# An mLSTM cell followed by a two-layer quick-GELU block: a copy placed ahead of a gelu on ScalarE, and two of GpSimd's adds given to VectorE

## The chip, the cores and the metric

The kernel runs on one core of a Trainium2 chip. The metric is the device time of one execution in microseconds; the time given for a kernel is the median of its runs.

## What is computed

An mLSTM cell runs over 768 steps for 4 batches of 8 heads of size 40. Its output becomes a matrix x of 3072 tokens by 320, which goes through two matrix products with a gelu between them:

```
h_tilde = einsum(C, q);  y = sigmoid(o_gate) * h_tilde / max(|n.q|, 1)      # C, n: the states with decay
x = y as (B*S, H*D)                                                        # 3072 x 320
h = x @ w_in                                                               # 320 x 2048
g = h * sigmoid(1.702 * h)
out = g @ w_out                                                            # 2048 x 320
```

All data are float32.

## The kernel before

**Stages.** The 768 steps are cut into six chunks of 128 steps, w = 0 to 5; a chunk has 4 x 128 = 512 tokens. For each chunk the loop at L929 runs a first product with its gelu (hidden features, up), and then a second product (down), into which the attention work of the next chunk is placed by a hand-written table (`attention`, L918). The order of the instructions on each engine is the order in which the program issues them: the schedule is manual, no planner moves anything. Each engine works through its own list in that order, and waits where an operand or a buffer isn't free.

**The first product.** Chunk 0 uses plain products (`up`, L614). Chunks 1 to 5 use `up_fast` (L707), which does a two-by-two block product with seven products in place of eight (a Strassen-Winograd form). The 2048 hidden features are eight pairs j = 0 to 7 of two rows of 128. For a pair, PE makes seven products of 256 columns (L722), each recorded as two matmuls: 14 for a pair. Their results lie in four PSUM banks: `p1`, `p56` (parts that are shared by the rows) and `row0`, `row1`. The rest of the inner dimension (the last 64 of 320) comes by `row_product` (L701); pairs 0 and 4 issue these matmuls for four pairs at once: their own, j + 2, j + 3 and then j + 1. A row is finished with its last matmul: for pairs 0 and 4 that is the first row product behind the pair, for odd pairs the pair's last L722, and for pairs 2 and 6 the rows are made ahead of `p1` and `p56`.

What happens to a pair's results:

- ScalarE copies the left half of `p1` into a buffer `parts` (L761), called the pair's part here. `parts` has two buffers, used in turn.
- VectorE makes the shared sums: `u2` (L762), a sum into `parts` (L763), a second sum into `parts` (L774).
- VectorE adds `row1` and `parts` into the second row of the pair's `g` (L775).
- The first row of `g`: in pairs 0 to 5 (`apart`) ScalarE copies `row0` into it (L739), and GpSimd adds the parts to it in place (L781), both inputs in SBUF. In pairs 6 and 7 VectorE adds from PSUM (L783).
- ScalarE applies the gelu in place, second row first and then the first row (`gelu_fast`, L688 to L690). This is issued one pair later: `up_fast(w, j)` issues the gelu of pair j - 1.

ScalarE's list in a pair is thus: the part (L761), the gelu of the pair in front (two L690), and the row copy (L739). In pair 2 alone the copy stands ahead of the part.

**Banks.** PSUM's eight banks are a pool of four single banks (`ps_m`) and a pool of two double ones (`ps_a`). The single ones go round: pair 4's `row0` and `row1` use the banks that pair 5 takes for `p1` and `p56`, and pair 5's rows use those that pair 6 takes for `p1` and `p56`. So a pair's `p1` waits for the row copy L739 of the pair in front, and its `p56` for that pair's L775. Rows of pairs 2, 3, 6 and 7 lie in the double banks.

**Other work in the same stage.** VectorE transposes blocks of k and q for the next chunk (L394: two behind pair 1, one behind pair 3, three behind pair 4, two behind pair 5). GpSimd makes differences of `g` for the fast second product (`hidden_difference`, L812, from pair 2 on; `hidden_sums`, L820 and L823, from pair 6 on). In chunk 1 alone GpSimd also makes four sums of the second product's weights (`weight_sums`, L803), one behind each of pairs 0 to 3. SyncE's queue loads the next chunk's v and k (L120).

**The second product.** `down_fast` (L831) makes seven products for half a chunk with PE (L844), sums up on VectorE (L847, L849), and makes late sums (L829). Its second product needs the gelus of pairs 4 to 7. Behind its fourth product, the next chunk's state product (L602) runs; it needs GpSimd's scaled values (L588), which need a column that ScalarE makes behind the last gelu. Later come the scores (L459, weighted on VectorE in L462) and the values (L503).

Of the kernel before, what the change touches and what calls it, by code (L numbers as in the profile page):

```python
# [12 lines left out]
OP = mybir.AluOpType  # L13
# [13 lines left out]
def kernel(  # L27
# [36 lines left out]
    op = ctx.enter_context(tc.tile_pool(name="op", bufs=2))  # L64
# [5 lines left out]
    V, A, G, T = nc.vector, nc.scalar, nc.gpsimd, nc.tensor  # L70
# [266 lines left out]
    def banks(name):  # L337
        return ps_a.tile([128, 2, 512], FP, tag="a", name=name)
# [349 lines left out]
    def gelu_fast(w, j):  # L688
        for i in (1, 0):
            A.activation(out=gs[w, j][:, i, :], in_=gs[w, j][:, i, :], func=AF.Gelu_apprx_sigmoid)  # L690
# [3 lines left out]
    def row_product(w, j, start):  # L694

        n = 2 if w == NW - 2 or (w == NW - 3 and j < 2) else 1
        for h in range(n):
            t = slice(h * W // n, (h + 1) * W // n)
            for i, row in enumerate(row_banks[w, j]):
                r = slice(i * 64, i * 64 + 64)  # L700
                T.matmul(row[:, t], w_in_x[r, j, :], xT[w][r, 2].rearrange("p b t -> p (b t)")[:, t],  # L701
                         start=(start and h == 0), stop=(not start and h == n - 1))

    def bank(name="p_h"):
        return ps_m.tile([128, W], FP, tag="m", name=name)

    def up_fast(w, j):  # L707

        x = temps[w]
        k = j % 4
        left, right = slice(0, half_w), slice(half_w, W)
        f = lambda c, i: w_in_sb[:, c, (2 * j + i) * 128:(2 * j + i + 1) * 128]

        def product(n, out, start, stop):
            a = {1: lambda: f(0, 0), 2: lambda: f(1, 0), 3: lambda: s_in[:, 2, j], 4: lambda: f(1, 1),  # L720
                 5: lambda: s_in[:, 0, j], 6: lambda: s_in[:, 1, j], 7: lambda: f(0, 1)}[n]()
            T.matmul(out, a, x[n], start=start, stop=stop)  # L722

        def row_0():
            product(2, row0[:, left], k == 0, False)
            product(3, row0[:, right], False, k > 0)

        def row_1():
            product(4, row1[:, left], k == 0, False)
            product(7, row1[:, right], False, k > 0)  # L730

        y = work.tile([L, 2, DM + 64], FP, tag="y", name="parts").rearrange("p a b -> p (a b)")
        u2 = second[w]
        g = gs[w, j] = gp.tile([128, 2, W], FP, tag="g", name="g")
        apart = j < NF // 2 - 2

        def copy_row():
            if apart:
                A.copy(out=g[:, 0, :], in_=row0)  # L739

        if k == 2:
            row0, row1 = row_banks[w, j]
            row_1()
            row_0()
        p1, p56 = bank(), bank()
        if k == 0:
            row0, row1 = row_banks[w, j] = bank(), bank()
        elif k != 2:
            row0, row1 = row_banks[w, j]
        product(1, p1[:, left], True, True)  # L750
        if k == 0:
            row_0()
        product(5, p56[:, left], True, True)
        product(6, p56[:, right], True, True)
        if k != 2:
            row_1()
        if k % 2:
            row_0()
        if k == 2:
            copy_row()  # L760
        A.copy(out=y[:, left], in_=p1[:, left])  # L761
        V.tensor_tensor(out=u2, in0=p56[:, right], in1=y[:, left], op=OP.add)  # L762
        V.tensor_tensor(out=y[:, 2 * half_w:3 * half_w], in0=p56[:, left], in1=u2, op=OP.add)  # L763
        if k == 0:
            row_product(w, j, False)
            for n in (2, 3):
                both = banks("p_h")
                row_banks[w, j + n] = both[:, 0, :], both[:, 1, :]
                row_product(w, j + n, True)
            row_banks[w, j + 1] = bank(), bank()  # L770
            row_product(w, j + 1, True)
        if j:
            gelu_fast(w, j - 1)
        V.tensor_tensor(out=y[:, half_w:2 * half_w], in0=row1[:, right], in1=u2, op=OP.add)  # L774
        V.tensor_tensor(out=g[:, 1, :], in0=row1, in1=y[:, half_w:3 * half_w], op=OP.add)  # L775
        u = y.rearrange("p (a t) -> p a t", t=half_w)[:, 0:3:2]
        g0 = g[:, 0, :].rearrange("p (a t) -> p a t", a=2)
        if apart:
            if k != 2:
                copy_row()  # L780
            G.tensor_tensor(out=g0, in0=g0, in1=u, op=OP.add)  # L781
        else:
            V.tensor_tensor(out=g0, in0=row0.rearrange("p (a t) -> p a t", a=2), in1=u, op=OP.add)  # L783

# [144 lines left out]
    for w in range(NW):  # L929
# [24 lines left out]
        else:  # L954
            token_sums(w)
            for j in range(NF // 2):
                up_fast(w, j)
                if more and j == 0:
                    gates(w + 1)
                    load(w + 1, "o")  # L960
                    if w == 1:
                        wait_for(ends[w + 1])
                if w == 1 and j < 4:
                    weight_sums(j)
                if more and j == 2:
                    columns_in(w + 1)
                    spread(w + 1)
                    load(w + 1, "vk")
                if more and j:
                    for n in ((0, 2), (), (4,), (6, 1, 3), (5, 7), (), ())[j - 1]:  # L970
                        block_transposes(w + 1, n)
                if more and j == 7:
                    columns_turn(w + 1)
                if 2 <= j < 6:
                    hidden_difference(w, j - 2)
                if j >= 6:
                    hidden_sums(w, (j - 6,), G)
# [54 lines left out]
```

## Time and profile before

| what | us |
|---|---|
| median of 3 runs (465.45 to 466.07) | 465.86 |
| the profiled execution | 465.77 |
| its span | 464.1 |
| PE busy | 456.6 (98%) |
| VectorE busy (DVE in the profile) | 349.2 (75%) |
| ScalarE busy (ACT) | 185.8 (40%) |
| GpSimd busy (POOL) | 162.8 (35%) |
| L781, GpSimd's add of the first row, 30 times | 38.2 |
| L739, ScalarE's copy of the first row, 30 times | 17.5 |
| L690, the gelus, 80 times | 47.8 |

All times in a profile are microseconds from the start of the span. A line of a timeline or of the chain gives the start, the length and then the instruction, "xN" when N of a kind are merged. An answer by stages gives for each stretch its length, the busy time of PE, PEld (weight loads), DVE, ACT and POOL with the number of instructions, then the granted TensorE clock (1.00 is full speed), the DMA engines' share, and GB/s. A line of waits gives who waited for whom, the sum, the number of times and the longest.

### The profile page before, as it was taken

The page shows a single profiled execution, that of the slowest core. Times are in us where ns is not written, and L with a number is a line of the kernel's source. Part 1 is how long each engine was busy: PE and PEld are TensorE (multiplying, and loading weights), DVE is VectorE, ACT ScalarE, POOL GpSimd, SP SyncE. Part 2 cuts the span into 40 slices and gives each one's busy share as a digit, 9 for nine tenths or more (in the row PEclk, how much of TensorE's full clock was granted, in tenths as well). Part 3 has the DMA queues.
Part 4 walks back from the last instruction along what each step waited for, and adds up shares of the span by engine and source line. Part 5 has one row for each costly group of instructions (what it writes and reads, how often), then busy time and mean ns, then how long its engine had stood idle before and what let it go on. Part 6 is the DMA issues. An engine that isn't in the chain of part 4 may idle for free.

```text
span 464.1 us, 12384 instructions
## 1 busy us (share of the span) xinstructions
PE 456.6 (98%) x5071; PEld 391.2 (84%) x5071; DVE 349.2 (75%) x738; ACT 185.8 (40%) x433; POOL 162.8 (35%) x154
## 2 busy tenths in 40 slices
PE   8999999999989999999999999999999999999996
PEld 6867877776859999779999779999888999787996
DVE  6788998799958785888786888787788766553722
ACT  5686779000536700455800354900264910164200
POOL 5101508000797700266800167610157710146200
PEclk9999999999989999999999999999999999999999
DMA  8998999049976025969024978315999305000000
GB/s 169 187 295 187 253 239 204 4 106 198 149 157 78 3 59 123 200 113 189 9 58 107 194 119 162 53 33 125 175 140 156 63 18 140 29 1 1 1 28 30
DMA packets 135561, 52.87 MB, mean 114 GB/s; under 512 B 101984, under 2 KB 131632, under 8 KB 135504
## 3 DMA queue, kind: packets, MB, share of 16 engines
q1 hardware_dynamic: 127136, 50.27, 55.4%
q10 hardware_dynamic: 8048, 1.66, 1.8%
q8 instruction: 40, 0.66, 0.6%
q0 software_dynamic: 320, 0.15, 0.2%
q14 instruction: 17, 0.14, 0.1%
HBM read 44.52 MB, written 7.54 MB: 112 GB/s over the span
## 4 chain that ended last, share of the span: by engine, by line
PE 88%; SPq 4%; DMA 2%; issue 2%; DVE 2%; POOL 1%; ACT 1%; DVEq 0%; POOLq 0%; ACTq 0%
PE p_out L844 33%; PE p_h L722 24%; PE p_out L790 8%; PE p_h L701 7%; PE p_h L626 5%; SPq L122 3%; PE p_c L602 3%; PE p_o L503 2%; PE p_s L459 2%; PE p_i L511 2%; DMA s_in<-in_moe_w_in_dram 2%; PE p_h L635 2%; POOL g L781 1%; SPq L167 0%; PE p_t L386 0%
## 5 line engine op out<-in xcount | busy, mean ns | idle before, releaser
L781 POOL TENSOR_TENSOR g<-g,parts 128x512 f32<-128x512 f32 x30 | 38.2, 1272 | 196.5 <-ACT g L739 187.7
L761 ACT COPY parts<-p_h 128x256 f32<-128x256 f32 x40 | 14.9, 372 | 164.5 <-PE p_h L722 134.1
L844 PE MATMUL p_out<-w_out_sb,g 128*128 128x160 f32 x480 | 68.9, 300 | 0.0
L722 PE MATMUL p_h<-xT,w_in_sb 128*128 128x256 f32 x240 | 66.4, 385 | 2.0 <-ACT g L739 2.0
L844 PEld LDWEIGHTS p_out<-w_out_sb,g 128*128 128x128 f32 x480 | 66.4, 190 | 0.5
L690 ACT ACTIVATE g<-g 128x512 f32<-128x512 f32 x80 | 47.8, 629 | 30.1 <-DVE g L775 19.1
L722 PEld LDWEIGHTS p_h<-xT,w_in_sb 128*128 128x128 f32 x240 | 44.9, 191 | 14.2 <-issue 5.5
L849 DVE TENSOR_TENSOR o_sb<-o_sb,p_out 128x160 f32<-128x160 f32 x70 | 21.4, 317 | 44.2 <-PE p_out L844 43.6
L844 PE MATMUL p_out<-t_sb,s 128*128 128x160 f32 x320 | 47.1, 300 | 0.0
L844 PEld LDWEIGHTS p_out<-t_sb,s 128*128 128x128 f32 x320 | 44.4, 190 | 0.2
L722 PE MATMUL p_h<-t_x,s_in 128*128 128x256 f32 x160 | 42.0, 385 | 0.0
L435 ACT ACTIVATE wt<-wt,cols 128x64 f32<-128x64 f32 x160 | 38.8, 334 | 0.1
L701 PE MATMUL p_h<-xT,w_in_x 64*128 64x512 f32 (+1 forms) x200 | 37.1, 514 | 0.0
L790 PE MATMUL p_out<-w_out_sb,g 128*128 128x320 f32 x128 | 35.7, 436 | 0.0
L722 PEld LDWEIGHTS p_h<-t_x,s_in 128*128 128x128 f32 x160 | 31.0, 194 | 4.4
L762 DVE TENSOR_TENSOR t_x<-p_h,parts 128x256 f32<-128x256 f32 x40 | 16.9, 424 | 20.3 <-PE p_h L722 12.9
L790 PEld LDWEIGHTS p_out<-w_out_sb,g 128*128 128x128 f32 x128 | 23.9, 190 | 9.6
L701 PEld LDWEIGHTS p_h<-xT,w_in_x 64*128 64x128 f32 x200 | 18.5, 186 | 14.9 <-issue 13.9
L739 ACT COPY g<-p_h 128x512 f32<-128x512 f32 x30 | 17.5, 582 | 31.1 <-PE p_h L701 17.5
L626 PE MATMUL p_h<-xT,w_in_sb 128*128 128x256 f32 x128 | 29.6, 384 | 0.0
L775 DVE TENSOR_TENSOR g<-p_h,parts 128x512 f32<-128x512 f32 x40 | 27.6, 691 | 1.4
L626 PEld LDWEIGHTS p_h<-xT,w_in_sb 128*128 128x128 f32 x128 | 23.6, 190 | 5.3 <-issue 2.4
(205 smaller groups left out, 853.6 us busy)
## 6 DMA issues: line engine op xcount, KB each, us to landing
q_sq<-in_q_dram SPq DMA_DIRECT2D x20, 320.0 KB, 10.6
wt<-m_row SPq DMA_DIRECT2D x20, 256.0 KB, 5.4
k_sq<-in_k_dram SPq DMA_DIRECT2D x16, 320.0 KB, 6.0
out_dram<-o_sb SPq DMA_DIRECT2D x24, 160.0 KB, 1.9
eo<-in_o_gate_dram SPq DMA_DIRECT2D x5, 640.0 KB, 7.9
bits<-in_moe_w_in_dram SPq DMA_DIRECT2D x6, 512.0 KB, 11.3
q_sq<-x_row SPq DMA_DIRECT2D x10, 256.0 KB, 3.0
v_st<-in_v_dram SPq DMA_DIRECT2D x14, 160.0 KB, 5.7
```

What stands on the lines that cost most here:

```text
L435: A.activation(out=x[:, h, :], in_=x[:, h, :], func=AF.Exp, scale=-1.0, bias=cols[w][:, c * PH + h:c * PH + h + 1])
L626: T.matmul(ph[j][i][:, t], w_in_sb[:, c, f * 128:(f + 1) * 128], x[:, c, t], start=(first and c == 0 and n == 0), stop=(not first and c == ...
L690: A.activation(out=gs[w, j][:, i, :], in_=gs[w, j][:, i, :], func=AF.Gelu_apprx_sigmoid)
L701: T.matmul(row[:, t], w_in_x[r, j, :], xT[w][r, 2].rearrange("p b t -> p (b t)")[:, t], start=(start and h == 0), stop=(not start and h == ...
L722: T.matmul(out, a, x[n], start=start, stop=stop)
L739: A.copy(out=g[:, 0, :], in_=row0)
L762: V.tensor_tensor(out=u2, in0=p56[:, right], in1=y[:, left], op=OP.add)
L775: V.tensor_tensor(out=g[:, 1, :], in0=row1, in1=y[:, half_w:3 * half_w], op=OP.add)
L781: G.tensor_tensor(out=g0, in0=g0, in1=u, op=OP.add)
L790: T.matmul(po, gs[w, f // 2][:, f % 2, b * L:(b + 1) * L], w_out_sb[:, f, :], start=(f == 0), stop=(f == NF - 1))
L844: T.matmul(po, a(f), b[:, f, :], start=(f == 0), stop=(f == NH - 1))
L849: V.tensor_tensor(out=dst, in0=x, in1=po, op=OP.add)
```

## The change

In `up_fast` the copy of the first row (L739) of pairs 0, 1, 3, 4 and 5 is issued ahead of the gelu of the pair in front, not behind it; pair 2's copy stays ahead of the part. In chunk 1 the adds L781 of pairs 4 and 5 are issued on VectorE in place of GpSimd, in the same position of the program: behind L775, ahead of the transposes. This holds for all five chunks in the first case and for two instructions in the second. Nothing is added or left out otherwise: no DMA, no buffer and no PE instruction moves. Line numbers behind this place are lower by one or so in the changed kernel.

```diff
         def copy_row():
-            if apart:
-                A.copy(out=g[:, 0, :], in_=row0)
+            A.copy(out=g[:, 0, :], in_=row0)
...
-        if k == 2:
+        if apart and k == 2:
             copy_row()
         A.copy(out=y[:, left], in_=p1[:, left])
...
             row_banks[w, j + 1] = bank(), bank()
             row_product(w, j + 1, True)
+        if apart and k != 2:
+            copy_row()
         if j:
             gelu_fast(w, j - 1)
         V.tensor_tensor(out=y[:, half_w:2 * half_w], in0=row1[:, right], in1=u2, op=OP.add)
...
         if apart:
-            if k != 2:
-                copy_row()
-            G.tensor_tensor(out=g0, in0=g0, in1=u, op=OP.add)
+            (V if w == 1 and j >= 4 else G).tensor_tensor(out=g0, in0=g0, in1=u, op=OP.add)
         else:
             V.tensor_tensor(out=g0, in0=row0.rearrange("p (a t) -> p a t", a=2), in1=u, op=OP.add)
```

## The prediction

> **What bounds the kernel now.** I read page part 1 first: PE is busy 456.6 of 464.1 us, so only two things can be won, PE's few gaps and matmuls that run slow. Cutting the trace into the five first products that follow the fast scheme, one per chunk (1 to 5), shows where both are. The columns are the busy times of PE, PEld, DVE, ACT, POOL, then the granted clock.
>
> ```profile
> 109.50:145.30 35.80, 33.76 (x147) 25.13 (x146) 28.38 (x59) 14.82 (x29) 26.74 (x18) 0.95 0.99 162
> 184.70:216.50 31.80, 31.80 (x146) 23.94 (x145) 27.88 (x57) 14.68 (x29) 15.28 (x13) 1.00 1.00 167
> 255.90:287.80 31.90, 31.90 (x155) 24.80 (x154) 27.97 (x57) 14.75 (x29) 15.34 (x13) 1.00 0.91 159
> ```
>
> The second chunk (w = 1) takes about 4 us more than the others for the same products. It differs by POOL, which has 11.6 us more work there (the four weight sums of L803, 2.9 us each). The waits of PE name the gap:
>
> ```profile
> PE p_h L722 <- ACT g L739: 2.0, 1, 2.0
> ```
>
> The chain that ended last shows how it comes about, and what it costs afterwards:
>
> ```profile
> 130.60 1.26 POOL g L812
> 131.87 1.25 POOL g L781
> 133.11 0.02 issue
> 133.14 0.63 ACT g L690
> 133.77 0.48 ACT g L739
> 134.25 0.04 issue
> 134.29 11.02 PE p_h L722 x42
> ...
> 207.28 9.26 PE p_h L722 x42
> ```
>
> Pair 5's first matmul needs the bank of pair 4's first row. ACT empties it (L739) only behind pair 3's gelu (L690), and that gelu waits for POOL's add (L781), late because POOL runs without a pause. PE stops for 2.04 us. The 42 matmuls behind the stop take 11.02 us, and 9.26 in the third chunk: 1.76 more. Three stretches of the stage show why:
>
> ```profile
> 132.20:134.30 2.10, 0.06 (x3) 0.01 (x1) 1.91 (x3) 1.10 (x2) 2.10 (x2) 1.00 0.61 237
> 134.30:137.70 3.40, 3.40 (x9) 2.72 (x10) 0.51 (x2) 0.90 (x2) 3.40 (x3) 0.54 1.21 210
> 137.70:145.30 7.60, 7.60 (x37) 6.68 (x36) 6.20 (x11) 3.76 (x8) 7.18 (x7) 0.98 1.23 144
> ```
>
> After the stop the clock is granted at about half for 3.4 us. So the stop costs 2.04 + 1.76 = **3.80 us**; the stages differ by 35.79 - 31.83 = 3.96 (chain, 109.52 to 145.31 against 184.71 to 216.54).
>
> **What the Trainium skill says.** "TensorE: Matmul & The Clock Gate", part 1, says the PE clock falls to half when a window of about 3.4 us was idle, and that the windows run freely. Here a stop of 2.04 us was enough, followed by 3.4 us at 0.54; I go by the trace: stop gone, half clock gone. "SBUF — State Buffer", section "Who interferes with whom", says that a VectorE instruction with two SBUF inputs and a GpSimd instruction that reads SBUF exclude each other for a whole instruction. The moved add (L781) has two SBUF inputs. The trace agrees: L829, also such an instruction, takes 0.42 us alone, but two took 1.62 beside POOL, whose instructions stand back to back:
>
> ```profile
> 152.11 1.62 DVE L829 TENSOR_TENSOR s<-g,s 128x256 f32<-128x256 f32 x2
> ```
>
> ```profile
> 149.82 2.75 POOL L588 TENSOR_TENSOR vw<-v_st,cols 128x656 f32<-128x656 f32 x2 [2.17 <-ACT cols L367]
> 152.54 1.79 POOL L579 TENSOR_TENSOR state_mid<-state,cols 128x328 f32<-128x328 f32 x2
> ```
>
> They end at 153.73, which is 0.27 us (256 elements' streaming) after the first L579 (about 153.45). The first was let in at the boundary at 152.54. So VectorE loses the rest of POOL's current instruction, then gets its turn.
>
> **Part 1, copy ahead of gelu, second chunk** (times on before's clock). Up to pair 3 little moves. The copy of pair 1 comes when its row is done (119.35), the table load (1.28) and pair 0's gelu behind it, so pair 2's left part moves from 121.80 to about 122.9; VectorE has transposes until 123.3 anyway. Pair 1's second gelu waits for POOL (123.68) as before, so pair 3's part starts at 124.3 as before. Pair 3's copy is ready at 125.5 to 126.1. As built, VectorE's L774 of pair 3 now waits for it; it would start at 126.1 anyway: 0. Pair 2's gelu still waits for POOL until 127.8, then comes pair 4's part at 128.35 (before 128.81). Pair 4's copy needs the row's last product: 1.16 us after the first L701 in the third chunk (203.58 to 204.74), so here 129.7 to 130.3, against 134.24 before. PE is free at 132.25. **The stop goes: -3.80.** The other bank that pair 5 needs is free at 130.9 (L775).
>
> **Part 2, two adds from POOL to VectorE.** POOL loses 2 x 1.27 us in this stage; it isn't what PE needs now. On VectorE a 128x512 add costs 0.61 (L783's spacing), if the port is free. Pair 4's add is issued at 130.8, 0.2 us after POOL's L812 took the port (130.60 to 131.86); it streams 0.53 (512 elements, scaled from 0.27) and ends at 132.4: 1.55 us in place of 0.61. Behind it are three transposes (2.96, end 135.25) and pair 5's four operations (2.0): L775 ends at 137.25. PE wants that bank for pair 6's second product at 132.2 + 3.02 + 1.73 + 0.43 = 137.4. **Cost 0, with 0.1 us to spare.** Pair 5's add (issued 137.15) meets another L812, about +0.9; two transposes end at 140.05. Then the remaining chain of VectorE, 5.12 us long in before (142.40 to 147.52), ends at 145.2, and the last gelu at 145.85 (148.18 before). PE leaves the stage at 141.5 and wants that gelu in its 29th matmul of L844, 3.80 later: 145.25. **A new stall of about 0.6.** Bounds: the two meetings with POOL cost 0 to 1.3 each; with none there is no stall, with both full it is 1.4.
>
> What follows is late by that stall at most: POOL's L588 would start at 147.45 and PE's L602, which needs it, at 150.8. Its loads (v_st, issued until 138.4, landing 5.6 to 8.4 us later) are there by 145.8. L462 before PE's L503 has only 0.1 us of slack in before (162.6 against 162.71); it hangs on VectorE and PE, which moved further than POOL, so I take 0, up to 0.8 if the port meeting falls badly. No DMA is moved and no queue of SP or POOL is passed.
>
> **Part 3, copy ahead of gelu, chunks 2 to 5.** Same working in the third chunk: pair 2's part 1.05 us later (197.9), VectorE 0.45 late in pairs 2 and 3, caught up in pair 4, where it had waited 0.93 for PE (204.78). The banks are free well before PE (row 5: copy ends 211.0, wanted 212.0). **0** each; bounds -0.1 and +0.3 for the four together.
>
> **Sum.** -3.80 + 0.6 = -3.2 us against the profiled execution (465.77 us; span 464.1, 1.7 outside). Its time is 0.09 under the median of the runs (465.86). 465.77 - 3.2 = **462.6**. Measurement tells about 0.2%, 0.93 us, from no change.
>
> **Rivals.**
> A, *the stop is removed whole*: VectorE misses POOL, no stall behind: 465.77 - 3.9 = **461.9**. For it: VectorE reaches L812 only 0.2 us after its start. Against: POOL is busy without a pause until 139.6, so some meeting is likely. It lies inside the main case's bounds.
> B, *the wait becomes one of VectorE*: the add of pair 4 loses one boundary more (POOL's L781 to 133.1) and ends at 133.65. Pair 6 then waits 1.2 us and the chain to the last gelu is 1.25 later: gain about 1.3, **464.5**. The same size comes if the slow clock stays without the stop: -2.04 + 0.6, 464.3.
> C, *slower*: POOL keeps the port across its next two instructions (L781 and the weight sum, to 136.0). The add ends at 136.5, three transposes and pair 5's operations at 141.35, PE waits 4.0 us for pair 6's second bank and the half clock (1.76) returns: the stage ends at 141.5 + 5.8 = 147.3, 2.0 after before: **467.7**. It decides from an end of the add after about 134.5: 2.1 us of stop plus 1.76 of clock then eat the gain. For it: POOL is never idle there and VectorE has only 0.1 us of slack. Against: L829 was let in at a boundary.
> D, *no effect*: pair 5 finds another reason to wait at 132.25. L775 (130.9) and the products say no: 465.8.
>
> **Chances.** Main case with A: 0.74 (range of its own 461.7 to 463.4). B: 0.12. C: 0.09. D: 0.05. B spans the border of 0.2%, two thirds faster. Faster 0.82, same 0.09, slower 0.09. The range takes in the main case and most of B: 461.7 to 464.6.
>
> **What would show it.** PE without a wait for L739 near 132, clock 1.00 through the stage, the stage near 32 us. L739 of pair 4 near 129.7. The moved add 1.2 to 1.6 us long, ended by POOL, not 0.68. A wait of PE of about 0.6 us for a gelu at L844 near 145. Wrong if PE waits for L775 at pair 6, if the half clock is still there, or if the chunks 2 to 5 take over 31.9 us in the stage.

## The result, and the profile after

The changed kernel takes 471.71 us (median of 4 runs, 470.48 to 472.40), the kernel before 465.65 beside it: a ratio of 1.0129, 95% interval 1.0104 to 1.0154. The forecast was 462.6, so sign and size are wrong; what came is the mechanism of rival C, held longer than C had priced it. The profiled execution takes 471.77 us (span 470.1), 6.0 more than that of before.

The same answer by stages as before, for the second and third chunk of after:

```profile
109.20:150.50 41.30, 35.07 (x146) 25.86 (x145) 38.83 (x63) 14.90 (x29) 26.56 (x17) 0.92 0.87 146
190.70:222.50 31.80, 31.80 (x145) 23.97 (x145) 27.91 (x57) 14.47 (x29) 15.28 (x13) 1.00 0.96 161
```

The third chunk is as before (31.80), and so are the later ones. The second has become longer, and it is now VectorE (third busy time) that is busy almost throughout, 38.8 us where it had 28.4; most of the difference is one instruction that waits, which the profile counts as busy. PE's waits have a new first line, and the one for the copy is gone:

```profile
PE p_h L722 <- DVE parts L762: 6.2, 1, 6.2
```

VectorE's timeline shows what that is:

```profile
130.62 0.69 DVE L776 TENSOR_TENSOR g<-p_h,parts 128x512 f32<-128x512 f32 x1
131.22 9.35 DVE L780 TENSOR_TENSOR g<-g,parts 128x512 f32<-128x512 f32 x1
140.50 1.09 DVE L394 STREAM_TRANSPOSE kT<-k_sq 128x512 f32<-128x512 f32 x1
...
143.78 0.42 DVE L762 TENSOR_TENSOR parts<-p_h,t_x 128x256 f32<-128x256 f32 x1
...
144.57 0.69 DVE L776 TENSOR_TENSOR g<-p_h,parts 128x512 f32<-128x512 f32 x1
145.18 0.68 DVE L780 TENSOR_TENSOR g<-g,parts 128x512 f32<-128x512 f32 x1
```

Pair 4's moved add (L780, before L781) took 9.35 us; pair 5's, with GpSimd idle, 0.68. GpSimd's timeline in the same stretch:

```profile
131.02 1.26 POOL L811 TENSOR_TENSOR g<-g 128x512 f32<-128x512 f32 x1
132.25 1.25 POOL L780 TENSOR_TENSOR g<-g,parts 128x512 f32<-128x512 f32 x1
133.47 2.88 POOL L802 TENSOR_TENSOR t_sb<-w_out_sb,t_sb 128x1280 f32<-128x1280 f32 x1
136.33 3.70 POOL L811 TENSOR_TENSOR g<-g 128x512 f32<-128x512 f32 x3
141.32 1.28 POOL L819 TENSOR_TENSOR s<-g 128x512 f32<-128x512 f32 x1 [1.29 <-ACT g L690]
```

Six instructions of GpSimd (L811, L780, L802, three L811) follow each other without a pause, each in its usual time. VectorE, waiting since 131.2, is passed at all five boundaries between them, and its add ends at 140.57, 0.54 us after GpSimd's list runs dry at 140.03. The list runs dry because L819 needs a gelu that itself waits for the held add. The chain that ended last carries it to PE:

```profile
129.02 1.11 PE p_h L701 x4
130.13 0.56 ACT g L738
130.70 0.54 ACT g L690
131.24 2.98 DVE g L780
134.21 6.29 issue
140.50 1.09 DVE kT L394
...
144.26 6.66 PE p_h L722 x18
150.92 8.69 PE p_out L843 x64
```

The 6.29 us named "issue" are the middle and end of the add: no semaphore event stands for a wait for the port (the way to SBUF that VectorE and GpSimd share, as the prediction has it). PE's stop in its own timeline, and the stretches around it by stages:

```profile
144.26 2.08 PE L722 MATMUL p_h<-t_x,s_in 128*128 128x256 f32 x4 [6.23 <-DVE parts L762]
```

```profile
138.10:144.30 6.20, 0.04 (x1) 0.04 (x1) 6.10 (x7) 0.89 (x2) 4.47 (x4) 0.86 1.27 142
144.30:147.70 3.40, 3.40 (x8) 2.77 (x9) 3.37 (x6) 1.60 (x3) 1.10 (x1) 0.50 0.40 66
```

The clock (third number from the end, 0.50 in the second line) is again at half behind the stop. Against before, the stop is 6.23 - 2.04 = 4.19 us longer. The 18 matmuls behind it take 6.66 us where 18 of 42 at full speed take 9.26 x 18 / 42 = 3.97, so slow matmuls cost 2.69 (before 1.76): 0.93 more. By the chains the stage starts 0.39 later (109.91 against 109.52), though nothing ahead of it was changed. These make 5.51 of the 5.61 by which the stage ends later (150.92 against 145.31); the rest of the 6.0 is lost behind the stage.

### The profile page after: what moved, and what is told of

Read it like the earlier page. It is cut to its first block, busy times and chain, and to the rows that moved or that the text cites. A ratio compares the mean times of both kernels' runs of the same rounds, so it can differ in the third digit from the quotient of the medians.

```text
span 470.1 us, 12389 instructions
## 1 busy us (share of the span) xinstructions
PE 458.2 (97%) x5071; PEld 392.3 (83%) x5071; DVE 357.4 (76%) x740; ACT 185.4 (39%) x433; POOL 160.1 (34%) x152
## 4 chain that ended last, share of the span: by engine, by line
PE 94%; DVE 3%; issue 2%; ACT 0%; DVEq 0%
PE p_out L843 33%; PE p_h L722 26%; PE p_out L789 7%; PE p_h L701 7%; PE p_h L626 6%; PE p_c L602 2%; PE p_o L503 2%; PE p_i L511 2%; PE p_s L459 2%; PE p_h L635 2%; PE p_t L386 1%; PE p_s L448 1%; DVE g L780 1%; PE p_w L415 1%; DVE state L579 0%
## 5 line engine op out<-in xcount | busy, mean ns | idle before, releaser
L780 POOL TENSOR_TENSOR g<-g,parts 128x512 f32<-128x512 f32 x28 | 35.6, 1273 | 197.1 <-ACT g L738 180.7
L843 PE MATMUL p_out<-w_out_sb,g 128*128 128x160 f32 x480 | 68.9, 300 | 0.0
L843 PEld LDWEIGHTS p_out<-w_out_sb,g 128*128 128x128 f32 x480 | 66.4, 190 | 0.5
L722 PE MATMUL p_h<-t_x,s_in 128*128 128x256 f32 x160 | 43.0, 393 | 6.2 <-DVE parts L762 6.2
L843 PE MATMUL p_out<-t_sb,s 128*128 128x160 f32 x320 | 47.2, 301 | 0.0
L843 PEld LDWEIGHTS p_out<-t_sb,s 128*128 128x128 f32 x320 | 44.4, 190 | 0.2
L435 ACT ACTIVATE wt<-wt,cols 128x64 f32<-128x64 f32 x160 | 38.8, 333 | 0.1
L738 ACT COPY g<-p_h 128x512 f32<-128x512 f32 x30 | 17.5, 582 | 52.3 <-PE p_h L701 26.2
L776 DVE TENSOR_TENSOR g<-p_h,parts 128x512 f32<-128x512 f32 x40 | 27.7, 692 | 1.4
```

What stands on the lines that cost most here:

```text
L435: A.activation(out=x[:, h, :], in_=x[:, h, :], func=AF.Exp, scale=-1.0, bias=cols[w][:, c * PH + h:c * PH + h + 1])
L780: (V if w == 1 and j >= 4 else G).tensor_tensor(out=g0, in0=g0, in1=u, op=OP.add)
L843: T.matmul(po, a(f), b[:, f, :], start=(f == 0), stop=(f == NH - 1))
```

## The experiments

Two questions: what each part of the change does alone, and why the add got no turn. P, C and D in the first four expectations are explained in them; theory C there isn't rival C of the prediction. For the second question the expectations use further letters. K: GpSimd's plain adds never give VectorE a turn. V: the form of VectorE's add (its operands) decides. S: the time that GpSimd has run since its last pause decides. W: something in this kernel's list decides. G, N and L are explained in the expectations that use them, H32 where it is tested. All kernels are the changed one with the edit shown, if nothing else is said.

### copy_only: the copies ahead, both adds on GpSimd

```diff
-            (V if w == 1 and j >= 4 else G).tensor_tensor(out=g0, in0=g0, in1=u, op=OP.add)
+            G.tensor_tensor(out=g0, in0=g0, in1=u, op=OP.add)
```

> The copies are moved as in the changed kernel, and all adds of the first row stay on GpSimd. Theory P (the add on VectorE, with both inputs in SBUF, gets no turn while GpSimd works without a pause; the copies' move does what was forecast): PE's stop before pair 5 and the half clock go, the second chunk's stage is near 32 us, and the time is 465.7 - 3.8 = 462 us. Theory C (the moved copies do the harm, by holding up the gelus behind them): the time stays near 471.

464.25 us (6 runs), ratio 0.9960 (0.9947 to 0.9974). The stop and the half clock are gone, but the gain is about half of the 3.8 us; the stage of this kernel:

```profile
109.50:143.30 33.80, 33.80 (x157) 25.60 (x156) 29.54 (x61) 14.66 (x29) 24.51 (x16) 1.00 0.93 154
```

PE enters the stage at 110.17 and leaves it at 142.17: 32.00 us against 35.79, which is 3.79 shorter. It leaves 3.14 us earlier than before, but the third chunk starts only 1.6 earlier (183.08 against 184.71). The rest goes behind the first product, where VectorE's and GpSimd's late sums meet; PE's two waits there for VectorE's L611 are 0.6 us of it, and what makes up the remainder wasn't traced. VectorE, then GpSimd:

```profile
147.55 3.45 DVE L822 TENSOR_TENSOR s<-s,g 128x512 f32<-128x512 f32 x2
```

```profile
148.72 3.43 POOL L588 TENSOR_TENSOR vw<-v_st,cols 128x656 f32<-128x656 f32 x2
```

Two L822 on VectorE take 3.45 us, and two L588 3.43 where before showed 2.75, which fits two engines that take the port in turn. So they do alternate here, and part 1 holds.

### adds_only: the adds on VectorE, the copies where they were

```diff
-        if apart and k != 2:
-            copy_row()
         if j:
             gelu_fast(w, j - 1)
...
+            if k != 2:
+                copy_row()
             (V if w == 1 and j >= 4 else G).tensor_tensor(out=g0, in0=g0, in1=u, op=OP.add)
```

> The two adds go to VectorE, and the copies stay where they were. Theory P: pair 4's add waits for the copy until 134.2 and then for GpSimd's list until it runs dry near 139.7; it ends near 140.2, PE stops again for about 5 us before pair 6, and the time is 471 to 472 us. Theory C: without the moved copies nothing is lost, about 465.7.

470.71 us (4 runs), ratio 1.0098 (1.0078 to 1.0117). VectorE's timeline, and then PE's waits:

```profile
134.71 5.90 DVE L781 TENSOR_TENSOR g<-g,parts 128x512 f32<-128x512 f32 x1 [3.02 <-ACT g L739]
```

```profile
PE p_h L722 <- DVE parts L763: 2.5, 1, 2.5
PE p_h L722 <- ACT g L739: 2.0, 1, 2.0
```

The old stop stays, and the add, though it arrives 3.5 us later, within a weight sum, is again held until GpSimd's list ends (140.06). The loss belongs to the moved adds. (Behind the second stop, of 2.48 us, the clock was 1.00 in the next 3.4 us, where before had 0.54 behind a stop of 2.04: a stop doesn't always bring the half clock.)

### pair5_only: only pair 5's add on VectorE

```diff
-            (V if w == 1 and j >= 4 else G).tensor_tensor(out=g0, in0=g0, in1=u, op=OP.add)
+            (V if w == 1 and j >= 5 else G).tensor_tensor(out=g0, in0=g0, in1=u, op=OP.add)
```

> As the changed kernel, but only pair 5's add goes to VectorE; in the changed kernel this add took 0.68 us, when GpSimd was idle. Theory P: now GpSimd still works when it is issued (near 136.7), so it is held until GpSimd's list stops for pair 5's gelu, near 143.4, some 7 us; the last gelus are late by about 6 us and PE waits for them in the second product: 470 us. Theory D (pair 4's add waited for something of its own, a buffer or a value, and not for the port): pair 5's add takes 0.7 to 1.6 us and the time is 462 to 463 us.

469.45 us (4 runs), ratio 1.0078 (1.0054 to 1.0101). VectorE and GpSimd:

```profile
136.22 6.54 DVE L780 TENSOR_TENSOR g<-g,parts 128x512 f32<-128x512 f32 x1
```

```profile
138.50 2.48 POOL L811 TENSOR_TENSOR g<-g 128x512 f32<-128x512 f32 x2
140.95 1.25 POOL L819 TENSOR_TENSOR s<-g 128x512 f32<-128x512 f32 x1
142.28 1.62 POOL L822 TENSOR_TENSOR s<-s,g 128x512 f32<-128x512 f32 x1
```

The add is passed at four boundaries and gets in between L819 (ends 142.20) and L822 (142.28), where GpSimd stands still for 0.08 us, because L822 reads what L819 has written. PE has no stop in the first product now, but it waits 3.8 us in the second one (L843) for gelus. This suggested that a pause of GpSimd lets VectorE in, and a bare boundary, where GpSimd's next instruction follows at once, doesn't.

### adds_psum: the two adds on VectorE, read from PSUM

The row of pairs 4 and 5 of the second chunk isn't copied; VectorE adds it from its bank, as in pairs 6 and 7.

```diff
-        apart = j < NF // 2 - 2
+        apart = j < NF // 2 - 2 and not (w == 1 and j >= 4)
```

> As the changed kernel, but VectorE makes pairs 4's and 5's adds as it makes those of pairs 6 and 7: the row is read from PSUM, and its copy is left out. One input is in SBUF. Theory P: such an add isn't held by GpSimd; both take 0.68 us, PE has no stop in the second chunk, 461.9 us. Theory D, and any theory in which VectorE simply has too much to do in this stage: an add of several us, or PE waiting for VectorE by 1 us and more, 464 us and above.

462.60 us (14 runs), ratio 0.9926 (0.9907 to 0.9944): the best version here. One input now lies in PSUM, and the add (L782) passes beside the same busy GpSimd. VectorE, then the chain:

```profile
136.86 0.68 DVE L782 TENSOR_TENSOR g<-p_h,parts 128x512 f32<-128x512 f32 x1
```

```profile
132.91 9.26 PE p_h L722 x42
142.17 8.69 PE p_out L843 x64
```

The Trainium skill, "SBUF — State Buffer", section "Who interferes with whom", says that a VectorE instruction with at most one SBUF input, outside its two-port modes, doesn't contend with GpSimd; 0.68 us here against 9.35 in after agrees. PE has no wait in the stage. (Two copies of ScalarE are left out as well, so not all of the gain over copy_only need be the adds'.)

### tail, tail2: the add against GpSimd's adds, with nothing else running

The kernel before, with tests behind its last store: GpSimd gets a list of additions in SBUF, VectorE some transposes and then one add of two SBUF inputs, so that it arrives in the middle of the list. In `tail` the lists have eight 128x512 instructions, in place, not in place, or with a broadcast input, and one add has 256 columns; `tail2` has lists in the kernel's order of 1280 and 512 columns.

```diff
+    for order, late in (((0, 1, 2, 3, 4, 5, 6) * 2, 12), ("B0B1B23B456", 15), ("B0B1B22B456", 15)):
+        A.copy(out=U[:, 0:1], in_=Q[5][:, 0:1])
...
+            G.tensor_tensor(out=x, in0=x, in1=y, op=OP.add)
+        for _ in range(late):
+            V.transpose(out=Q[5], in_=Q[4])
+        add_512()
```

> The kernel before, with seven tests behind its last store (so it takes longer; nothing of the result is left out). In each test GpSimd makes eight instructions of 128x512 in a row, VectorE makes transposes and then one add with both inputs in SBUF, whose length is read. GpSimd's instruction and VectorE's delay differ: 1 plain adds in place, VectorE arriving in the first; 2 the same, arriving in the third; 3 the same, arriving in the sixth; 4 plain adds to another place; 5 a second input that is broadcast; 6 as 4 with a 256-element add of VectorE; 7 as 4, where the sixth of GpSimd's reads what the fifth wrote. Theory K (kind: GpSimd's plain adds, back to back, give no turn, and those with a broadcast input or none do): the add takes as long as GpSimd's list is in 1, 2, 3, 4 and 6 (10, 7, 3.5, 7, 7 us), up to 1.8 us in 5, and in 7 it ends behind the fifth, some 3 to 4 us. Theory S (a turn is lost only long after GpSimd's last pause): up to 1.8 us in 1, 2, 4, 5, 6 and 7, long at most in 3. Theory V (it lies in VectorE's add of 512 elements in two pieces): long wherever this add is used, 5 included, and short in 6.

> The kernel before with three further tests behind its last store (nothing of the result is left out). 1: fourteen plain 128x512 instructions of GpSimd in a row, VectorE's add arriving in the eighth. 2: GpSimd's order of the changed kernel (128x1280 and 128x512 in turn, eleven in all), VectorE arriving in the sixth, 11 us after the pause. 3: as 2, but the seventh reads what the sixth wrote, a pause. Theory S: long in 2 (until the list ends, about 7 us) and perhaps in 1, about 1.6 us in 3. Theory W (it lies in something else of the changed kernel, such as the waits for other engines between GpSimd's instructions): up to 1.8 us in all three.

One run of each (527.9 and 515.2 us with the tests). In the first test of both kernels list and add didn't meet. In the six others of `tail` and the two others of `tail2` VectorE got in at the first boundary: 0.46 to 1.28 us, and 1.64 and 1.71. (At the boundary of the last one GpSimd paused, because its seventh instruction reads what the sixth wrote.) This refutes K and V. S fell too: in `tail2` the add arrived 11 us behind the start of a list that had not paused. W was left.

### gap, gap_ws0, gap_ws1: a pause in GpSimd's list

A copy of one column on GpSimd that reads what the instruction ahead of it wrote, so that GpSimd must stand still for an instant: behind the first difference (`gap`), the first weight sum (`gap_ws0`) or the second one (`gap_ws1`). The copied value is used nowhere. The edit of `gap_ws1`:

```diff
                 if w == 1 and j < 4:
                     weight_sums(j)
+                    if j == 1:
+                        wait_for(t2[:, 0, :])
```

> The changed kernel, with one tiny copy on GpSimd (128x1) behind the first difference (L811) of the second chunk, which reads what that difference wrote, so that GpSimd pauses for less than 0.1 us. Theory G (any pause in GpSimd's list is enough for VectorE's add to get its turn): pair 4's add ends behind the difference, 1.5 to 1.8 us long in place of 9.35; pair 5's add may still wait for GpSimd's list, some us. If both are short the time is 462 to 463 us; if pair 5's isn't, 466 to 470. Theory N (the add wants GpSimd's list to stop for longer): still 9 us and 471 to 472.

> The changed kernel, with the tiny copy on GpSimd and its pause behind the first weight sum (near 122.8), five instructions and 8 us ahead of the moved add. Theory S (VectorE loses its turn only when GpSimd has run for long, or for many instructions, since its last pause; four of 512 elements were harmless): between the known cases, so the add is either 1.6 us long (463 to 464 us for the kernel) or some 9 us (471). Theory L (only a pause in the very neighbourhood, while VectorE waits, lets it in): 9 us, 471 to 472.

> As gap_ws0, with the pause behind the second weight sum (near 127), three instructions and 4.1 us ahead of the moved add. Theory S: the add takes its turn at the first boundary, 1.6 us, and the kernel 463 to 464 us. Theory L: 9 us and 471 to 472.

463.50 us (8 runs), 463.58 (4) and 463.39 (4); ratios 0.9940 (0.9918 to 0.9962), 0.9957 (0.9931 to 0.9983) and 0.9968 (0.9932 to 1.0004); the last interval just takes in no change. `gap`, GpSimd, then VectorE, then PE's wait:

```profile
131.72 1.26 POOL L811 TENSOR_TENSOR g<-g 128x512 f32<-128x512 f32 x1
133.04 0.54 POOL L592 COPY mark<-g 128x1 f32<-128x1 f32 x1
```

```profile
131.91 1.62 DVE L780 TENSOR_TENSOR g<-g,parts 128x512 f32<-128x512 f32 x1
...
138.24 1.22 DVE L780 TENSOR_TENSOR g<-g,parts 128x512 f32<-128x512 f32 x1
```

```profile
PE p_out L843 <- ACT g L690: 0.7, 1, 0.7
```

A pause of 0.06 us (132.98 to 133.04), and the stage is as the prediction had it: adds of 1.62 and 1.22 us, a stall of 0.7 for a gelu. The second add got in at a bare boundary. In `gap_ws1` and `gap_ws0` the pause lies 4.3 and 8.4 us ahead of pair 4's add (127.2 and 123.2), and VectorE still gets in at the next bare boundary (1.76 and 1.03 us, 1.75 and 1.07). So the pause needn't be long (as in N) nor coincide with the wait (as in L); it changes what comes after it.

### gap_ws1_32, gap_nowait, no_mark: partitions, or the pause

H32 supposed that the list's first copy is to blame: it covers 32 partitions, which might leave GpSimd's parts out of step until a pause brings them together. `gap_ws1_32` makes the pausing copy as narrow, `no_mark` leaves the first copy out (its value is used nowhere; GpSimd then starts earlier and waits for pair 1 from 119.0 to 122.8), and `gap_nowait` has the narrow copy of `gap_ws1_32` at the same place, reading an old column, so that there is no pause. The edits of the two narrow copies, and then of `no_mark`:

```diff
+                    if j == 1:
+                        wait_for(t2[0:32, 0, :])        # gap_ws1_32
+                        wait_for(ends[w + 1])           # gap_nowait, in its place
```

```diff
-                    if w == 1:
-                        wait_for(ends[w + 1])
```

> As gap_ws1, but the one-column copy on GpSimd that reads the second weight sum covers 32 partitions where it covered 128. Theory H32 (an instruction on 32 partitions leaves GpSimd's parts running out of step, so that the port is never free on all partitions at a boundary until a pause brings them back into step): pair 4's add takes about 9 us again, to the end of GpSimd's list, and the run about 471 us. Rival (any pause behind the list's start is enough, whatever its partitions): the adds take 1.76 and 1.0 us as in gap_ws1, and the run 463.4.

> The changed kernel without the copy of one column over 32 partitions with which GpSimd's list of the second chunk begins (it holds GpSimd until the chunk in front has got far enough; its value is used nowhere). GpSimd's list starts some 4 us earlier. H32: pair 4's add is let in at the next boundary, 0.7 to 1.8 us, and the run takes 462 to 466 us. Rival (a long unbroken list keeps VectorE out whatever it began with): the add takes until the list pauses, several us, and the run 469 us or more.

> As gap_ws1_32, with the same one-column copy on GpSimd at the same place behind the second weight sum, but reading the column that the list's first copy reads, which has long been there, so that nothing makes GpSimd pause. If the pause is what lets VectorE in, pair 4's add takes about 9 us and the run about 471 us, as in the changed kernel. Rival (any change of GpSimd's list, or the few tenths of a us by which it moves, is enough): the add takes at most 1.8 us and the run about 463.5.

| | us (runs) | ratio, interval | pair 4's add |
|---|---|---|---|
| gap_ws1_32 | 463.77 (9) | 0.9953, 0.9936 to 0.9971 | 1.76 us |
| no_mark | 464.90 (18) | 0.9976, 0.9965 to 0.9987 | 1.71 us |
| gap_nowait | 472.99 (2) | 1.0134, 1.0082 to 1.0186 | 9.49 us |

GpSimd in `gap_ws1_32`, and in `gap_nowait`:

```profile
125.12 2.89 POOL L802 TENSOR_TENSOR t_sb<-w_out_sb,t_sb 128x1280 f32<-128x1280 f32 x1
128.07 0.17 POOL L592 COPY mark<-t_sb 32x1 f32<-32x1 f32 x1
...
133.53 1.73 POOL L780 TENSOR_TENSOR g<-g,parts 128x512 f32<-128x512 f32 x1
```

```profile
125.16 2.91 POOL L802 TENSOR_TENSOR t_sb<-w_out_sb,t_sb 128x1280 f32<-128x1280 f32 x1
128.02 0.18 POOL L592 COPY mark<-both 32x1 f32<-32x1 f32 x1
...
133.47 1.26 POOL L780 TENSOR_TENSOR g<-g,parts 128x512 f32<-128x512 f32 x1
```

The two kernels differ in what one 0.17 us copy reads. In the first it starts 0.06 us after the end of the weight sum (128.01), and later VectorE gets between two instructions: L780 takes 1.73, not 1.26. In the second it starts before the record of the weight sum ends (128.07), nobody gets in, and by the ratios the run is some 8 us longer. The moment of the meeting isn't it: the add arrives 0.05 us behind the start of GpSimd's L811 in the first, 0.06 us in the second. H32 is refuted, by `gap_ws1_32` (`no_mark` came out as H32 had said, but it has a pause too); what decides between these two is whether GpSimd pauses once behind the copy with which its list begins. The wait in `no_mark` does the same; that kernel's own loss of 1.1 us, against `gap_ws1_32`, is as large as a wait of PE for L762 (1.1 us in its list of waits).

### tail3, tail4: the same, outside the kernel

Tests as in `tail`, each list with a copy of one column over 32, 64, 96 or 128 partitions at its head and no pause inside. `tail4` has 20 such tests behind a void one, and was run twice (`tail4_again`). The edit of `tail4`:

```diff
+    for first in [slice(0, p) for p in (128,) + (64, 128, 64, 32) * 5]:
...
+        G.tensor_copy(out=mark[first], in_=U[first, 0:1])
+        for n in range(8):
+            G.tensor_tensor(out=P[n], in0=P[n], in1=U[:, 0:512], op=OP.add)
```

> The kernel before with seven tests behind its last store, in which nothing else runs: GpSimd copies one column over 128, 128, 32, 32 (the last 32), 64, 96 and 128 partitions, then does eight additions of 128x512 in SBUF back to back; VectorE does four transposes and then one addition of two SBUF inputs, which arrives in about the third of the eight. The first test only warms up. H32: the addition takes up to the end of the eight, about 7 us, behind the copies over 32, 64 and 96 partitions, and at most 1.8 us behind those over 128. Rival (the copy's partitions do not matter): at most 1.8 us in all seven.

> The kernel before with 21 tests like those of tail3 behind its last store: first a void one, then five times a list whose first copy covers 64, 128, 64 and 32 partitions. If the 64 partitions made the long addition of tail3, all ten additions behind such a copy take about 7 us and all others at most 1.8. If it was chance, a few additions of the twenty are long, with no order in the partitions. A third way: none is long.

> The same kernel as tail4, once more. If chance decides each test, other tests are long than in tail4; if something fixed in the program does, the same ones.

One run each (533.4, 683.5 and 681.6 us with the tests; in `tail3` the first test was void as well). The long addition was met outside the kernel. VectorE's timeline of `tail4`, two tests next to each other:

```profile
501.03 1.32 DVE L1011 TENSOR_TENSOR s_in<-s_in 128x512 f32<-128x512 f32 x1
511.70 7.43 DVE L1011 TENSOR_TENSOR s_in<-s_in 128x512 f32<-128x512 f32 x1
```

One of six adds was long in `tail3` (7.42 us), two of 20 in `tail4`, none of 20 in `tail4_again`; all others took 1.32 to 1.46. The three long ones stood behind a copy over 64 partitions, but 18 more such lists let VectorE in (8 in `tail4`, 10 in `tail4_again`). So 64 partitions don't force it (whether they favour it, three cases can't tell), and the same program does it in one execution and not in the next. In each long test VectorE was passed at every boundary up to the end of the list, never at some only.

**What stays open.** Why a list starts out closed to VectorE. In the tests a list without a pause was open in 50 of 53 meetings (the one at a pause, in `tail2`, isn't counted). In the kernel the list that starts with the copy at about 120 us, and doesn't pause behind it, was closed in all four profiles in which a moved add meets it (after, adds_only, pair5_only, gap_nowait). Behind one more pause it was open in all five (gap, gap_ws0, gap_ws1, gap_ws1_32, no_mark). The times say the same of the runs that have no profile: all 14 of the four kernels took 468.91 us or more, all 43 of the five took 467.11 or less. No list was seen to change from one to the other without a pause. That a pause sets the state anew, mostly to open, would fit all of this; it is argued, not shown, and what makes this kernel's list start out closed so regularly, and whether its first copy has a part in it, isn't known.

## Why the prediction was wrong

**Part 1, the stop goes: -3.80.** Right. In copy_only PE has no stop and no half clock, and the stage is 3.79 us shorter (32.00 against 35.79). In after pair 4's copy (L738) runs from 130.11 to 130.69; the stage starts 0.39 later than in before, so on before's clock that is 129.72 to 130.30, against a forecast of 129.7 to 130.3. (Of the 3.79 us copy_only loses 1.5 again behind the stage; adds_psum, whose stage also ends at 142.17, doesn't.)

**Part 2, pair 4's add "ends at 132.4 ... Cost 0, with 0.1 us to spare".** Wrong, and it is the step that failed. It rested on "VectorE loses the rest of POOL's current instruction, then gets its turn". In after the add got no turn at five boundaries and ended at 140.57. The inference came from one meeting, L829 beside L588, which lay right behind a pause of GpSimd of 2.17 us. (Another in before, L829 beside L439 at 158.90, was as fair, and lay behind a pause of 1.38.) The list that the add would meet had run without a pause for 11. The runs show both outcomes for bare boundaries, so fair meetings elsewhere couldn't vouch for this one. The skill's rule, that the two exclude each other for a whole instruction, was read as a wait for one instruction of GpSimd; in after the add waited through five more.

**"With 0.1 us to spare": also misread, though it didn't decide.** The prediction, and the paragraph on banks that stands ahead of it, let pair 6's second product wait for pair 5's L775 (L776 in after). In after PE starts again at 144.26, just behind the end of L762 (144.20) and ahead of the start of L776 (144.57); the stops in adds_only and gap_nowait end with the same operation. So the bank comes free about 1.05 us earlier than was counted, and the room was about 1.2 us. That wasn't enough for an add that ended some 8 us late.

**"Bounds: the two meetings with POOL cost 0 to 1.3 each."** Wrong for the same reason: 1.3 is one instruction of GpSimd. The upper bound was the end of its list, at 139.6 in before, which the prediction itself gave as the time to which "POOL is busy without a pause". With no line of the profile that bounds the wait, the range should have reached beyond C.

**The remaining sizes.** Where VectorE gets its turn, part 2 comes out as forecast: in gap 1.62 us against 1.55, then a stall of 0.7 against 0.6, and a ratio of 0.9940 (0.9918 to 0.9962) against a forecast 462.6 / 465.77 = 0.9932. The three other kernels with a pausing copy gained a little less (0.9953 to 0.9968). The stall's match is in part luck: taken as written, pair 5's add (issued 137.15, 0.61 long, 0.9 more for the port) and two transposes of about 2.0 us end at 140.7, and not at 140.05, which would make the stall about 1.2; in gap the port cost this add 0.6 (1.22 against 0.61).

**Part 3, 0 in chunks 2 to 5.** Right: 31.80 us in after's third chunk, with PE busy throughout, and 31.9 at most in the others.

**Rivals.** C named the mechanism, at 0.09, and stopped it at 136.0 behind the weight sum; three differences more make 140.03. It priced the wait of PE at 4.0 us and the clock at 1.76, measured 6.23 and 2.69. The 4.0 rests on the misread bank, which makes it about 1.05 too long, and on an end of the add 4.1 us too early. The clock's share isn't a fixed price: in gap_nowait a stop of 6.36 us was followed by 18 matmuls in 5.83 us, which is 1.86 more than at full speed. B was the neighbouring size of the same thing. A and D didn't happen.

## What to carry to other kernels

Moving an operation from GpSimd to VectorE takes work from GpSimd's list but, with two SBUF inputs, can make VectorE wait for that same list; bound the wait by the list's next pause or end, which is what it came to in the kernels that lost, and not by one instruction. An operand that can be read from PSUM takes the instruction out of this contest, and saves the copy as well (adds_psum, 0.9926). Fair meetings of the two engines elsewhere in a trace don't vouch for a new one, and tests outside the kernel don't either: 50 of 53 let VectorE in at the next boundary, while by the times all 14 runs of the four kernels above held it. What settled the question here was the kernel itself, with one pause more or with the operand elsewhere.

## What the runs showed of the hardware

- A VectorE add with two SBUF inputs was passed at five boundaries in succession (9.35 us), with GpSimd's instructions at their usual lengths.
- A pause of GpSimd of 0.06 us, up to 8.4 us ahead of the meeting, was enough for the add to take 1.62 to 1.76 us in place of 9.35 to 9.49. A copy without a pause left it at 9.49.
- The same add with one input in PSUM took 0.68 us beside the same busy GpSimd.
- The same test program held two of 20 adds for 7.43 us in one execution, and none in the next.
- The granted clock was 0.54 in the 3.4 us behind a stop of PE of 2.04 us (before), and 1.00 in the 3.4 us behind one of 2.48 us (adds_only).
- Waiting for the port has no line of its own in the profile: the waiting instruction looks long and busy, and the chain calls most of it "issue".
